# Sixteen gate steps moved beside the first exponentials of an S4 + SwiGLU kernel

## The chip, the cores and the metric

The kernel runs on one core of a Trainium2 chip. It is one launch: forward and backward pass of a block with a state-space layer (S4) and a gated feed-forward layer (SwiGLU). Time is device time in microseconds (us), the median of the runs shown. The engines are TensorE (PE, matrix products, with PEld for loading its weights), VectorE (DVE), ScalarE (ACT, activations from tables), GpSimd (POOL) and SyncE (SP, which issues DMAs). Each engine works through its own instructions in the order in which they stand in the program. Products land in PSUM, everything else lives in SBUF (128 partitions) or in DRAM.

## The reference

Sequence length L = 2048, width D = 576, state N = 128, hidden width F = 4608. Cut to what matters:

```python
xn = layernorm(x)                                   # eps 1e-5
logdA = dt * A;  dB = dt * B                        # D x N, complex
P  = exp(logdA[:, :, None] * l)                     # l = 0 .. L-1
K  = einsum("dn,dnl,dn->dl", C, P, dB).real         # the kernel of the convolution
s  = irfft(rfft(xn, 2L) * rfft(K, 2L))[:L] + xn * Dskip
h  = silu(xn @ w1) * (xn @ w3)                      # gate and up products
out = x + s * silu(h @ w2)
# outputs: out, and the gradients of 12 inputs for a given grad_out
```

## The kernel before

**Stages.** The program has five stretches. (1) Set-up: loads, statistics of the layer norm, selectors and angles. (2) Exponentials: the real part of P is built from powers of a base, so 36 chunks of 16 channels need 54 exponentials of 128x1024 in all; beside them stand the normalisation of x, its transposes, and the spectra of xn. (3) Generation: 36 chunks (`kgen_chunk`, `kgen_sum`) compute sines, multiply them with the exponentials, and sum over N into `KT`. (4) Convolution: two halves (`conv_half`) of four blocks each, products of spectra. (5) The output product (`ffn_output`), the backward pass and the gradients of the inputs.

**The gate steps.** `ffn_hidden` computes gate and up products in 72 steps: 9 blocks of 512 hidden channels (`fb`) times 8 pairs of token tiles. One step has 20 matmuls (L901 for the four full slices of D, L909 for the 64-row tail of both weights), then on ACT silu (`s_t`, L913), a copy of the first tile's gate (`g_t`, L917) and two copies of the up product (`u_t`, L918), on DVE the copy of the second tile's gate (L915) and the product `h_t` (L920). SP stores `h_t`, POOL's queue stores `g_t` and `u_t` for the backward pass. `g_t`, `u_t`, `s_t` and `h_t` have three buffers each, the PSUM tiles `pg` and `pu` two.

**What sets the order.** A scheduler places every instruction by a priority, a time in microseconds written in the source: `pre(us)` in the prologue (us × 600) and `at(us)` after it (100000 + us × 1000). `Chain` makes the instructions of DVE, ACT and POOL in the prologue follow each other in the order written. `ffn_hidden` draws chunks from the generator `ssm_forward` whenever their time is due (`due <= T`), so that a gate step every 6 units of `at` (48 for the 8 of a block) stands against a chunk every 8. The pools of `ffn_hidden` are opened after the prologue has closed its own.

**The prologue.** `ln_load` reads even token tiles straight; odd ones are needed with their rows reversed, so they go through a DRAM copy `odd["A_u"]`, written reversed by one DMA and read back. `ln_stats` takes statistics of all 16 tiles, then one square root on ACT. `ln_normalise` transposes 8 tiles at a time into `ln_pt`; a DMA doubles the last 64 rows. `early_exps` writes e_ps (L514, two PSUM buffers), the exponential (all recorded at the helper's line L72) writes a third of a 128x3072 tile `E_k` (three buffers), and SP stores 18 of these. `early_spectra` computes 128 products of 288 columns (L533, `u_ps`) and DVE copies them (L537). `split3` writes values split into three bfloat16 pieces to `PCS_dram`; those of the base rows come back as `lhs_r`, the operand of the e_ps products. POOL computes the weights Wr and Wi of the sum. `dft_phases` wraps angles on DVE. In generation, L589 and L590 are the products and sines of a chunk (`et_ps` to `cs_k`), L626 its sum (`kps`), L630 the copy to `KT`, one per chunk. In the convolution, ACT copies spectra of KT into `kraw` (L729) and inverse transforms into `ev` (L843), and DVE multiplies.

The core of a gate step (q is the tile of the pair):

```python
nc.scalar.activation(out=s_t[:, :, q, :], in_=pgv, func=ACT.Silu)                      # L913
if q % 2 == 1:
    nc.vector.tensor_copy(out=g_t[:, :, q, :], in_=pgv)                                # L915
else:
    nc.scalar.copy(out=g_t[:, :, q, :], in_=pgv)                                       # L917
nc.scalar.copy(out=u_t[:, :, q, :], in_=pu[:]...)                                      # L918
# after both tiles
nc.vector.tensor_tensor(out=h_t[:]..., in0=s_t[:], in1=u_t[:], op=ALU.mult)            # L920
```

Of the kernel before, what the change touches and what calls it, by code (L numbers as in the profile page):

```python
# [76 lines left out]
class K:  # L77

# [47 lines left out]
    def setup_consts(self):  # L126
# [8 lines left out]
        self.eps_col = const.tile([P, 1], FP32, name="eps_col")  # L135
        nc.vector.memset(self.eps_col[:], 1e-5)
# [8 lines left out]
    def pre(self, us):  # L145
        self.tc.cur_priority = int(us * 600)
# [9 lines left out]
    def ln_load(self, sb):  # L156
        nc, cfg = self.nc, self.cfg
        xf = self.aps["A_u"].flatten_outer_dims()
        self.xs, self.xts = [], []
        for b in range(cfg.LT // 4):  # L160
            xt = sb.tile([P, 4, cfg.D], BF16, name=f"xt{b}")
            rows = xf[4 * b * P:4 * (b + 1) * P, :].rearrange("(i two p) d -> two p i d", two=2, p=P)
            nc.sync.dma_start(out=xt[:, 0:4:2, :], in_=rows[0])
            self.xs += [xt[:, i, :] for i in range(4)]
            self.xts.append(xt)
        for b, xt in enumerate(self.xts):
            nc.sync.dma_start(out=xt[:, 1:4:2, :], in_=self.odd["A_u"][2 * b:2 * b + 2].rearrange("i p d -> p i d"))

    def ln_stats(self, sb, small):
        nc, cfg = self.nc, self.cfg  # L170
        D, LT = cfg.D, cfg.LT
        half = D // 2
        self.mv = sb.tile([P, LT, 2], FP32, name="mv")
        for i in range(LT):
            stats = small.tile([P, 2, 6], FP32, name="stats")
            self.V.bn_stats(stats[:, 0, :], self.xs[i][:, 0:half])
            self.V.bn_stats(stats[:, 1, :], self.xs[i][:, half:D])
            if i > 0:
                self.V.bn_aggr(self.mv[:, i - 1, :], last[:])
            last = stats  # L180
        self.V.bn_aggr(self.mv[:, LT - 1, :], last[:])
        sd = sb.tile([P, LT], FP32, name="sd")
# [3 lines left out]
    def ln_normalise(self, sb, ps):  # L186
        nc, cfg = self.nc, self.cfg
        D, LT, DT = cfg.D, cfg.LT, cfg.DT
        nfull = D // P
        rem = D - nfull * P  # L190
        negmr = sb.tile([P, LT], FP32, name="negmr")
        self.V.scalar_tensor_tensor(out=negmr[:], in0=self.mv[:, :, 0], scalar=-1.0, in1=self.rstd[:], op0=ALU.mult,
                                       op1=ALU.mult)
        TB = 8
        for tb in range(0, LT, TB):
            for i in range(tb, tb + TB):
                self.V.tensor_scalar(out=self.xn_bf[:, i, :], in0=self.xs[i], scalar1=self.rstd[:, i:i + 1],
                                        scalar2=negmr[:, i:i + 1], op0=ALU.mult, op1=ALU.add)
            if tb > 0:
                self.dft_rows()  # L200
            tsl = slice(tb * P, (tb + TB) * P)
            for c, (do, dsz) in enumerate(cfg.dch):
                pt = ps.tile([P, TB * P], BF16, name="ln_pt")
                for j in range(TB):
                    nc.tensor.transpose(pt[:dsz, j * P:(j + 1) * P], self.xn_bf[:, tb + j, do:do + dsz],
                                        self.ident_bf[:])
                self.V.tensor_copy(out=self.xnT[:dsz, c, tsl], in_=pt[:dsz, :])
            nc.sync.dma_start(out=self.xnT[rem:P, nfull, tsl], in_=self.xnT[0:rem, nfull, tsl])
        for b in range(LT // 4):
# [54 lines left out]
    def prologue(self, matp, selp, xp):  # L264
# [6 lines left out]
        self.rstd = self.persist.tile([P, LT], FP32, name="rstd")  # L271
        self.xnT = xp.tile([P, DT, L], BF16, name="xnT")
        self.PCS_dram = self.dram.tile([3, 3, D, N], BF16, name="PCS_dram")
        mul = lambda e, o, a, b: e.tensor_tensor(out=o[:], in0=a[:], in1=b, op=ALU.mult)
        with pool(name="par_tmp", bufs=1) as tmp, pool(name="sel_tmp", bufs=1) as st, pool(name="ln_sb", bufs=1) as lsb, \
                pool(name="ln_small", bufs=4) as small, pool(name="dftgen", bufs=1) as dg, \
                pool(name="ex_l", bufs=1) as lp, pool(name="ex_e", bufs=3) as ep, pool(name="ex_u", bufs=2) as up, \
                pool(name="ex_ps", bufs=2, space=PS) as eps, ExitStack() as early:
            lps = early.enter_context(pool(name="ln_ps", bufs=2, space=PS, side="right"))
            self.V, self.S, self.G = (Chain(self.tc, e) for e in (nc.vector, nc.scalar, nc.gpsimd))  # L280
            self.pre(0)
            irow = st.tile([P, 512], I32, name="irow_i")
            nc.gpsimd.iota(irow[:], pattern=[[1, 512]], base=0, channel_multiplier=0)
            self.dma_engines, self._dma_i = [nc.sync, nc.scalar], 0
            self.odd = {n: self.dram.tile([LT // 2, P, D], BF16, name="odd_" + n) for n in ("A_u", "grad_out", "out_0", "out_1")}
            logdt = self.load_dvec(tmp, aps["A_log_dt"], "logdt", fill=0.0)
            nc.sync.dma_start(out=self.odd["A_u"][:], in_=self.turned(aps["A_u"].flatten_outer_dims()))
            self.pre(0.5)
            self.A_re = self.load_dmat(tmp, aps["A_A_re"], "A_re", fill=-1.0)
            self.ln_load(lsb)  # L290
            self.pre(1)
            SELR = self.selector_values(st)
            LR_ = lp.tile([P, D // 16, N], BF16, name="lhs_r")
# [3 lines left out]
            self.dt_col = self.persist.tile([P, DT], FP32, name="dt_col")  # L297
            self.pre(3)
            self.S.activation(out=self.dt_col[:], in_=logdt_f[:], func=ACT.Exp)
            self.dma_engines = [nc.sync]  # L300
            self.load_rates(tmp)
            self.selector_casts(st)
            dt_b = self.dt_col[:, :, None].to_broadcast([P, DT, N])
# [4 lines left out]
            self.S.copy(out=self.irow[:], in_=irow[:])  # L308
            self.dft_angles()
            for k, eng in enumerate((nc.sync, self.S, nc.sync)):  # L310
                ld = eng.dma_start(out=LR_[k * 16:(k + 1) * 16],
                                   in_=self.PCS_dram[2, k].rearrange("(k p) n -> p k n", p=16))
            self.pre(8)
            self.build_reader(SELR, st)
            self.pre(10)
# [1490 lines left out]
```

## Time and profile before

| what | us |
|---|---|
| median of 3 runs | 1880.09 |
| lowest and highest run | 1870.91 and 1883.1 |
| the profiled execution's own time | 1874.95 |
| its span, first to last instruction | 1873.2 |
| set-up | 0 to 36 |
| exponentials, until the first gate product | 36 to 127.0 |
| until the first sine of generation | 127.0 to 152.3 |
| generation, until the last copy to KT | 152.3 to 433.8 |
| convolution, until the last h_t | 433.8 to 602.3 |
| output product, backward, gradients | 602.3 to 1873.2 |

| engine | busy us | share of the span |
|---|---|---|
| PE | 1689.1 | 90% |
| DVE | 1370.1 | 73% |
| ACT | 910.0 | 49% |
| POOL | 352.1 | 19% |

How to read it: the profile shows one execution. Its span leaves out 1.75 us around the first and last instruction. An instruction is named by engine, line and the tiles that it writes and reads ("PE L901 pg<-wmB_w,xnT"). Groups give count, busy time, mean duration in ns and the idle time of the engine just before them with what ended it. Ends of matmuls are modelled, so that a busy PE need not be a PE at its peak; starts are recorded. Stage borders in the first table are starts and ends of named instructions, so they can be read off the same events in another profile.

### The profile page before, as it was taken

The numbers are of one execution on the slowest core, as the hardware profiler recorded it, in microseconds if no ns is written. First come the engines' busy times: TensorE is split into PE (matmuls) and PEld (weight loads), VectorE is DVE, ScalarE is ACT, GpSimd is POOL, SyncE is SP. The second block draws the span as 40 slices with busy tenths as digits, with TensorE's granted clock in tenths as the row PEclk, the third lists the DMA queues.
The fourth block names the chain that finished last, engine by engine and source line by source line (L and its number), as shares of the span: only waits on it lengthen the run. The fifth ranks groups of instructions, "written<-read, shape, count | busy, mean of one in ns | idle before, by whom it ended". The sixth has DMA issues, their size and how long they took to land. (4 is left out here: it accounts for less than half of the span.)

```text
span 1873.2 us, 38325 instructions
## 1 busy us (share of the span) xinstructions
PE 1689.1 (90%) x15461; PEld 1231.2 (66%) x15516; DVE 1370.1 (73%) x2081; ACT 910.0 (49%) x1632; POOL 352.1 (19%) x567
## 2 busy tenths in 40 slices
PE   2999999999897999799999999999998968979997
PEld 0335555555353777578878887888777756868786
DVE  5538666768988555588694989759998954867675
ACT  3768888887563111465765756565444300001001
POOL 4021222222223111011111111111110242031032
PEclk9999999999998999899999999999999998989999
DMA  6579988887777997658666575579999899988993
GB/s 172 175 242 328 328 304 305 308 291 267 239 242 225 218 205 179 218 157 232 183 198 190 180 211 173 167 210 284 258 233 232 179 221 245 209 195 204 220 210 72
DMA packets 627231, 417.27 MB, mean 223 GB/s; under 512 B 424429, under 2 KB 567853, under 8 KB 622445
## 3 DMA queue, kind: packets, MB, share of 16 engines
q1 hardware_dynamic: 569820, 281.98, 58.3%
q0 software_dynamic: 30672, 106.50, 16.8%
q10 hardware_dynamic: 26560, 26.35, 4.7%
q8 instruction: 121, 1.98, 0.4%
q14 instruction: 58, 0.47, 0.1%
HBM read 135.74 MB, written 190.89 MB: 174 GB/s over the span
## 5 line engine op out<-in xcount | busy, mean ns | idle before, releaser
L1657 PEld LDWEIGHTS <-acts 128*128 128x128 bf16 x2304 | 228.4, 100 | 100.7 <-DMA acts<-GG_dram 19.8
L1610 PEld LDWEIGHTS <-xn_bf 128*128 128x128 bf16 x2304 | 225.6, 98 | 37.0 <-issue 10.1
L1229 DVE TENSOR_TENSOR pr_q<-et_ps,pz 128x1024 f32<-128x1024 f32 x144 | 176.0, 1222 | 48.9 <-PE et_ps L1224 41.8
L1657 PE MATMUL px<-wT,acts 128*128 128x288 bf16 x1408 | 182.5, 289 | 17.3 <-DMA wT<-in_B_w_dram 17.3
L901 PEld LDWEIGHTS <-xnT 128*128 128x128 bf16 x1152 | 107.4, 98 | 115.5 <-issue 25.3
L1232 DVE TENSOR_REDUCE S_all<-pr_q 128x32 f32<-128x1024 f32 x144 | 175.3, 1217 | 3.4
L1552 PE MATMUL ph<-w2T,goT 128*128 128x256 bf16 x1440 | 173.0, 275 | 1.6 <-ACT gh L1555 1.4
L901 PE MATMUL pg<-wmB_w,xnT 128*128 128x512 bf16 x526 | 147.9, 382 | 16.4 <-DVE g_t L915 9.5
L901 PE MATMUL pu<-wmB_w,xnT 128*128 128x512 bf16 x571 | 155.4, 379 | 0.4
L1590 PE MATMUL pgw<-go_o,h_n 128*128 128x288 bf16 x1152 | 150.4, 287 | 4.1 <-DVE h_n L1530 2.8
L1552 PEld LDWEIGHTS <-goT 128*128 128x128 bf16 x1440 | 140.4, 99 | 19.7 <-issue 2.8
L1610 PE MATMUL pgw<-gu_n,xn_bf 128*128 128x256 bf16 x1152 | 135.6, 276 | 7.0 <-ACT gw L1594 6.8
L1657 PE MATMUL px<-wA,acts 128*128 128x288 bf16 x896 | 123.4, 298 | 19.6 <-DMA acts<-GG_dram 19.1
L1590 PEld LDWEIGHTS <-h_n 128*128 128x128 bf16 x1152 | 112.6, 98 | 32.5 <-DVE h_n L1530 3.3
L1610 PE MATMUL pgw<-gg_n,xn_bf 128*128 128x256 bf16 x1152 | 130.2, 273 | 1.6 <-ACT gw L1612 1.6
L913 ACT ACTIVATE s_t<-pg 128x512 bf16<-128x512 f32 x144 | 87.8, 610 | 89.4 <-PE pu L909 44.7
L1685 ACT ACTIVATE go<-gx 128x576 bf16<-128x576 f32 x16 | 10.9, 683 | 220.7 <-DVE gx L1668 220.7
L1555 ACT CAST gh<-ph 128x512 bf16<-128x512 f32 x144 | 82.0, 600 | 71.6 <-PE ph L1552 54.0
L590 ACT ACTIVATE cs_k<-et_ps 128x512 bf16<-128x512 int16 x216 | 112.1, 643 | 1.7 <-PE et_ps L589 1.3
L1612 ACT CAST gw<-pgw 128x256 bf16<-128x256 f32 x144 | 53.9, 375 | 99.3 <-PE pgw L1610 96.7
L924 POOL DMA_DIRECT2D G_dram<-g_t x72 | 52.3, 727 | 232.3 <-DVE g_t L915 223.9
L918 ACT CAST u_t<-pu 128x512 bf16<-128x512 f32 x144 | 86.9, 604 | 12.0 <-PE pu L901 12.0
(302 smaller groups left out, 3232.2 us busy)
## 6 DMA issues: line engine op xcount, KB each, us to landing
U_dram<-u_t POOLq DMA_DIRECT2D x72, 256.0 KB, 4.3
G_dram<-g_t POOLq DMA_DIRECT2D x72, 256.0 KB, 4.0
H_dram<-h_t SPq DMA_DIRECT2D x72, 256.0 KB, 4.7
Q_dram<-q_k SPq DMA_DIRECT2D x36, 512.0 KB, 4.2
h_n<-U_dram POOLq DMA_DIRECT2D x18, 1024.0 KB, 8.7
gg_n<-G_dram POOLq DMA_DIRECT2D x18, 1024.0 KB, 5.9
GU_dram<-gu_n SPq DMA_DIRECT2D x36, 512.0 KB, 3.6
GG_dram<-gg_n SPq DMA_DIRECT2D x36, 512.0 KB, 8.3
```

Of the source, the lines that this page charges most:

```text
L590: nc.scalar.activation(out=CS[:, :, o:o + 256], in_=pt[:].bitcast(I16)[:, :, 0::2], func=ACT.Sin, scale=6.283184 / 2 ** 16)
L901: ins = nc.tensor.matmul(pt[:], lhsT=xnT[:, c, ts], rhs=wm[w][:, c, :], start=(q == 0 and c == 0), stop=(q == 1 and c == nfull - 1))
L913: nc.scalar.activation(out=s_t[:, :, q, :], in_=pgv, func=ACT.Silu)
L918: nc.scalar.copy(out=u_t[:, :, q, :], in_=pu[:].rearrange("p (g f) -> p g f", g=ng))
L1229: nc.vector.tensor_tensor(out=pr[:].rearrange("p r k e -> p r (k e)"), in0=T[h][:].rearrange("p k z d a -> p (k z d a)")[:, None].to_broad ...
L1232: nc.vector.tensor_reduce(out=self.S_all[:, :, d0:d0 + 4], in_=pr[:].rearrange("p r k (d a) -> p (r k) d a", d=4), op=ALU.add, axis=AX.X)
L1552: self.pe_last = nc.tensor.matmul(ph[j][:, k, :].rearrange("p (a f) -> p a f", f=P), lhsT=lw, rhs=rh, start=(n == 0), stop=(n == nfull))
L1555: self.sc(lambda: nc.scalar.copy(out=gh[:, j], in_=ph[j][:]))
L1590: self.pe_last = nc.tensor.matmul(pgw[pi_][:, 0:pw], lhsT=hn[:, tt, fl * P:(fl + 1) * P], rhs=go_o[:, tt, po:po + pw], start=(tt == 0), st ...
L1610: self.pe_last = nc.tensor.matmul(pw_[:, 0:FG], lhsT=self.xn_bf[:, tt, c * P:(c + 1) * P], rhs=nat[:, tt, :], start=(tt == 0), stop=(tt == ...
L1612: self.sc(lambda: nc.scalar.copy(out=gw[:, c], in_=pw_[:, 0:FG]))
L1657: self.pe_last = nc.tensor.matmul(px[pi_][:, 0:pw], lhsT=act[:, ai, fi, :], rhs=w[:, po:po + pw], start=(n == 0), stop=(n == len(steps) - 1))
```

## The change

- **Gate steps among the exponentials.** `EARLY = 16`: the pools of `ffn_hidden` are opened ahead of the prologue, and its first 16 steps are placed among the exponentials; from step 4 on, the first product of step n follows the product of exponential 4n − 13. For block 0 the token tiles are taken in another order (even ones first), weights come over POOL's queue, and the stores of g and u go in one DMA for each of two groups of channels. The later 56 steps are tied to marks: 38 over the 36 chunks (the first ahead of chunk 0), 9 in each half of the convolution.
- **Silu by tanh in these steps.** silu(g)·u = (0.5 + 0.5·tanh(g/2))·g·u: ACT computes tanh into a float32 tile, POOL the product g·u, DVE the rest. All sines, and silus of later steps, are ordered after the last exponential.
- **g copies.** Steps 0 to 3 and those in the convolution have both g copies on ACT; the other early ones have both on DVE; in between, DVE takes q = 1 and a third of q = 0.
- **Layer norm.** Odd tiles are loaded straight and reversed by a product with a flipped identity and copied back by ACT; the DRAM copy of x moves to the start of generation. Statistics, root and normalisation are done for even tiles, then for odd ones; the root is a bit trick with three Newton steps on DVE, so ACT's square root is gone. Tail rows are transposed twice by matmuls instead of doubled by a DMA. Transposes, flips and spectra share a pool of two one-bank PSUM tiles (`t_ps`).
- **Exponentials.** One PSUM buffer instead of two, tiles of 128x1024 with four buffers, 54 stores instead of 18, `E_dram` laid out by pairs of chunks. Spectra are copied in pieces of 288 columns (64 instead of 32 casts).
- **Queues.** The writes of the base rows and their return go over ACT's queue, the other pieces of `split3` over SP's (were POOL's); `dft_phases` moves from DVE to POOL; `load_rates` comes later. Priorities of the prologue (× 1000 instead of × 600), of generation and of the convolution's blocks are new.

The diff, cut to its core:

```diff
-        self.tc.cur_priority = int(us * 600)
+        self.tc.cur_priority = int(us * 1000)
...
+    def ln_flip(self, ps):
+        for t in range(1, self.cfg.LT, 2):
+            for h in range(2):
+                cols = self.xs[t][:, h * H:(h + 1) * H]
+                pt = ps.tile([P, 512], FP32, name="t_ps")
+                nc.tensor.matmul(pt[:, 0:H], lhsT=self.flip_bf[:], rhs=cols, start=True, stop=True)
+                self.S.copy(out=cols, in_=pt[:, 0:H])
...
-        self.S.activation(out=sd[:], in_=self.mv[:, :, 1], func=ACT.Sqrt, bias=self.eps_col[:], scale=1.0)
-        self.V.reciprocal(out=self.rstd[:], in_=sd[:])
+        self.root(small, self.rstd[:, sl], self.mv[:, sl, 1], len(tiles))
...
+    def root(self, small, y, var, n):
...
+        for _ in range(3):
+            V.scalar_tensor_tensor(out=a[:], in0=y, scalar=-0.5, in1=y, op0=ALU.mult, op1=ALU.mult)
+            V.tensor_tensor(out=a[:], in0=a[:], in1=v[:], op=ALU.mult)
+            V.scalar_tensor_tensor(out=y, in0=a[:], scalar=1.5, in1=y, op0=ALU.add, op1=ALU.mult)
...
-                pool(name="ex_l", bufs=1) as lp, pool(name="ex_e", bufs=3) as ep, pool(name="ex_u", bufs=2) as up, \
-                pool(name="ex_ps", bufs=2, space=PS) as eps, ExitStack() as early:
+                pool(name="ex_l", bufs=1) as lp, pool(name="ex_e", bufs=4) as ep, pool(name="ex_u", bufs=2) as up, \
+                pool(name="ex_ps", bufs=1, space=PS) as eps, pool(name="t_ps", bufs=2, space=PS) as tps:
...
-            self.dma_engines, self._dma_i = [nc.sync, self.S], 0
+            self.dma_engines, self._dma_i = [self.S], 0
             self.split3(tmp, rho, 2)
...
+            self.ln_flip(tps)
+            self.dft_sines()
+            even, odd = [*range(0, LT, 2)], [*range(1, LT, 2)]
+            self.pre(12)
+            self.ln_stats(even, small)
+            self.ln_normalise(even, tps)
+            self.early_exps(SELR, LR_, ep, eps, 0, 2)
+            self.pre(24)
+            self.ln_stats(odd, small)
+            self.ln_normalise(odd, tps)
...
-            self.dma_engines = [nc.gpsimd]
+            self.dma_engines = [nc.sync]
             self.split3(tmp, thr, 0)
             self.split3(tmp, th64, 1)
...
+            self.early_spectra(up, tps, 46, 1.1)
+            self.exps_last = self.S.prev
+            for n in range(self.EARLY + 1):
+                next(gate)
...
-            E = ep.tile([P, 2, TW], BF16, name="E_k")
...
+                E = ep.tile([P, 1024], BF16, name="E_k")
                 pe = ps.tile([P, 1024], FP32, name="e_ps")
...
+                self.exps.append(self.e_last)
+                self.S.activation(out=E[:], in_=pe[:], func=ACT.Exp)
+                nc.sync.dma_start(out=self.E_dram[c2 // 2, :, o:o + 1024], in_=E[:])
...
+            with self.tc.issue_after(self.exps_last.ins):
+                nc.scalar.activation(out=CS[:, :, o:o + 256], in_=pt[:].bitcast(I16)[:, :, 0::2], func=ACT.Sin,
+                                     scale=6.283184 / 2 ** 16)
+        self.marks.append(ins)
...
+    def gate_mark(self, n):
+        i = n - self.EARLY
+        if i < 38:
+            return 36 * i // 38 - 1
+        h, k = divmod(i - 38, 9)
+        return 36 + 8 * h + (-1 if k == 0 else (1, 3, 4, 4, 5, 5, 6, 6)[k - 1])
...
+            ld = nc.sync if fb else nc.gpsimd
...
+                pair = [4 * (n % 4) + n // 4 + 2 * q for q in range(NT)] if fb == 0 else [NT * n, NT * n + 1]
+                early = step < self.EARLY
...
+                                        if early:
+                                            lead = self.exps[4 * step - 13] if step >= 4 else None
+                                        else:
+                                            lead = self.marks[mark] if mark >= 0 else None
...
-                    nc.scalar.activation(out=s_t[:, :, q, :], in_=pgv, func=ACT.Silu)
-                    if q % 2 == 1:
+                    if early:
+                        nc.scalar.activation(out=th[:, :, q, :], in_=pgv, func=ACT.Tanh, scale=0.5)
+                    else:
+                        with self.tc.issue_after(self.exps_last.ins):
+                            nc.scalar.activation(out=s_t[:, :, q, :], in_=pgv, func=ACT.Silu)
+                    if step < 4 or step >= self.EARLY + 38 or (not early and q == 0 and step % 3):
+                        nc.scalar.copy(out=g_t[:, :, q, :], in_=pgv)
+                    else:
                         nc.vector.tensor_copy(out=g_t[:, :, q, :], in_=pgv)
...
+                if early:
+                    nc.gpsimd.tensor_tensor(out=s_t[:], in0=g_t[:], in1=u_t[:], op=ALU.mult)
+                    nc.vector.tensor_scalar(out=hv, in0=th[:], scalar1=0.5, scalar2=0.5, op0=ALU.mult, op1=ALU.add)
+                    nc.vector.tensor_tensor(out=hv, in0=hv, in1=s_t[:], op=ALU.mult)
+                else:
+                    nc.vector.tensor_tensor(out=hv, in0=s_t[:], in1=u_t[:], op=ALU.mult)
...
-            k.prologue(matp, selp, xp)
+            gate = k.ffn_hidden(wp, gup, fps)
+            k.prologue(matp, selp, xp, gate)
...
-                k.ffn_hidden(wp, gup, fps, 0, 12, k.ssm_forward(0, 8, 8))
+            k.ssm = k.ssm_forward(21, 7.3, 1)
+            for _ in gate:
+                pass
```

More of the change, by code (lines that the diff above doesn't have):

```diff
@@ L169, in ln_stats @@
[L169 to L174, printed above, removed]
+        self.xts = [sb.tile([P, 4, cfg.D], BF16, name=f"xt{b}") for b in range(cfg.LT // 4)]
+        for k in range(2):
+            for b, xt in enumerate(self.xts):
+                rows = xf[4 * b * P:4 * (b + 1) * P, :].rearrange("(i two p) d -> two p i d", two=2, p=P)
+                nc.sync.dma_start(out=xt[:, k:4:2, :], in_=rows[k])
@@ new lines, in ln_load, with ln_stats @@
+        self.xs = [xt[:, i, :] for xt in self.xts for i in range(4)]
+    def ln_flip(self, ps):
+        nc, H = self.nc, self.cfg.D // 2
+        for t in range(1, self.cfg.LT, 2):
[4 more added lines that the diff above has]
+                self.S.copy(out=cols, in_=pt[:, 0:H])
+    def ln_stats(self, tiles, small):
+        half = self.cfg.D // 2
+        last = None
+        for i in tiles:
@@ L210, in ln_normalise, with ln_fold @@
+    def ln_fold(self):
+        for b in range(self.cfg.LT // 4):
             lo, hi = self.xn_bf[:, 4 * b:4 * b + 2, :], self.xn_bf[:, 4 * b + 3:4 * b + 1:-1, :]
```

315 lines of the change are left out of this document (166 added, 149 removed).

## The prediction

> **What bounds the kernel now.** I first read the page's busy digits in 40 slices of 46.8 us, then busy time in windows cut at events of the trace, then the timelines and groups inside them.
>
> ```profile
> PE   2999999999897999799999999999998968979997
> DVE  5538666768988555588694989759998954867675
> ACT  3768888887563111465765756565444300001001
> ```
>
> TensorE (PE) is at 9 nearly throughout, but that is one reading over stages with different limits. The windows (us, busy time and instruction count per engine, granted clock, DMA share, GB/s) are: exponentials, generation of the kernel, convolution, and everything after.
>
> ```profile
> 36.00:127.00 91.00, 85.17 (x271) 26.42 (x270) 39.33 (x73) 65.45 (x69) 12.83 (x17) 1.00 0.58 197
> 152.30:433.80 281.50, 272.10 (x3599) 153.09 (x3635) 199.82 (x276) 244.21 (x485) 68.25 (x94) 1.00 0.89 310
> 433.80:602.30 168.50, 148.72 (x836) 76.70 (x849) 157.66 (x216) 94.04 (x197) 39.67 (x54) 0.96 0.73 237
> 602.30:1873.00 1270.70, 1157.80 (x10625) 962.28 (x10622) 931.67 (x1401) 486.55 (x853) 210.00 (x371) 0.97 0.81 204
> ```
>
> Between the first and second lie 25.3 us, up to the first sine. PE bounds generation (272 of 281.5), VectorE (DVE) the convolution (157.7 of 168.5). The exponentials also look PE-bound, but that PE is slow. In PE's timeline (start, duration, count):
>
> ```profile
> 126.05 1.14 PE L533 MATMUL u_ps<-xt,cCS 128*128 128x288 bf16 x4
> 126.98 0.63 PE L901 MATMUL pg<-wmB_w,xnT 128*128 128x512 bf16 x1
> ...
> 130.01 1.04 PE L901 MATMUL pg<-wmB_w,xnT 128*128 128x512 bf16 x4
> ...
> 134.11 1.04 PE L901 MATMUL pg<-wmB_w,xnT 128*128 128x512 bf16 x4
> ...
> 136.06 0.65 PE L533 MATMUL u_ps<-xt,cCS 128*128 128x288 bf16 x4
> ```
>
> The same four 288-column products take 1.14 us before the first gate product at 126.98 and 0.65 after it; single starts lie 240 ns apart before 127. The window prints clock 1.00, yet these spacings are half speed: the printed clock can't be used there. So 85 us of PE work is about 43 at full rate, and ACT waits for it:
>
> ```profile
> ACT E_k L72 <- PE e_ps L514: 40.5, 37, 17.2
> ```
>
> **Part 1: generation loses gate steps.** A gate step (two token tiles, 20 products) is 130.01 to 134.11, 4.10 us of PE. Of 72, three finish before 152.3, 45 in generation, 24 after (counted by h_t). Copies of KT mark chunks:
>
> ```profile
> L630 ACT CAST KT<-kps x3: 402/403/403, 250.2 to 267.7; 128x256 bf16<-128x256 f32 x3
> ```
>
> They start at 250.20, 256.96 and 267.72: a chunk with one gate is 6.76 us, with two 10.76, so a further gate is 3.95 to 4.1. Check: 36 × 6.8 + 9 × 3.95 = 280.4, measured 281.5. The changed order holds 17 gates ahead of the first sine, 37 among the 36 chunks and 18 in the convolution. Hence 36 × 6.8 + 3.95 = 248.8, **−32**. The bound below: DMA moves 281.5 us × 310 GB/s = 87 MB here; 8 steps fewer take off 8 × 0.77 MB, and 81 MB at those 310 GB/s would need 262 us, −20. Two slices of the page reach 328, which gives 247, so I keep −32. The bound above is chunks at 2.7 + 4.0 throughout, −34. Late next is ACT: 244.2 less 8 gates × 3.0 (two each of 0.61, 0.60 and one of 0.58) = 220 of 249, and DVE, which takes over every third first g copy, 199.8 + 12 × 0.68 − 8 × 1.35 = 197; PE stays last.
>
> **Part 2: the convolution loses gate steps and copies.** DVE pays for every gate:
>
> ```profile
> L915 DVE CAST g_t<-pg 128x512 bf16<-128x512 f32 x24 | 16.2, 677 | 1.2 <-ACT s_t L913 1.2
> L920 DVE TENSOR_TENSOR h_t<-s_t,u_t 128x1024 bf16<-128x1024 bf16 x24 | 16.1, 671 | 0.3 <-ACT u_t L918 0.3
> ```
>
> Six gates fewer save 6 × 1.35 = 8.1 us, the g copies moved to ACT 18 × 0.68 = 12.2: 20.3. DVE then holds 137 us, plus its 11 of waits, so 148 to 150: I take **−18**. ACT gains 18 × 0.58 and loses 6 × 3.0, 94 to 86; PE falls to 149 − 24 = 125; neither binds. The bounds are −25 (the new places also fill DVE's waits of 5.1 and 3.5 us for kraw and KT) and −10 (ACT copies delay kraw and ev, for which DVE waits already).
>
> **Part 3: the prologue gains gate steps.** Its end, the first sine, is now at 152.3.
> - PE at full rate: 17 × 4.1 = 70; 54 pairs of exponents × 0.45 = 24; 128 spectra products × 0.12 = 15.6; transposes and flips 7; W 1.4: 118 us. Products could begin when the even half is normalised: its statistics are half of 15.2 us, root 13 × 0.16 = 2.1 (by DVE's smallest rows, 0.15 to 0.19), eight at 0.42; with the loads about 40. So 158 if PE never waits.
> - ACT: 54 × 1.025 = 55.4; 16 × 2 tanh at silu's 0.61 and 2 u copies at 0.60 = 38.8; g copies of four steps 4.7; W 4.5; one table load 1.3: 105 from about 46, so 151. The two engines are close; neither fully hides the other.
> - DVE: before's 39 + later g copies 12 × 2 × 0.68 = 16, plus h work 16 × (0.68 + 0.68) = 22, plus smaller casts and early statistics: about 96, covered by 125.
> - Two exponent buffers become one: a pair then waits for the exponential before it. Such a turn-round has no row; lower bound 0 (ACT does a tanh or a copy meanwhile), upper 0.8 × 54 = 43 (pair 0.45 plus hand-over). Most exponentials alternate with gate work; 5.
> - POOL gets a product 128x1024, estimated 1.39 × 1024/640 = 2.2 us from its W products, plus 2 to 4 DMA issues of 0.73: at most 5.1 of each step's about 7, covered. W's eight products (11 us) and the selectors stand in its order between two gates' stores: with three g_t buffers a stall of 0 to 10; 4.
> - SP carries 54 stores of 256 KB instead of 18 of 768, the H stores, spectra, and split pieces moved from POOL. An H store waits for DVE, which waits for POOL; exponential stores stand behind it, four buffers deep, then the exponential itself. 0 if on time, 48 if each of 16 costs 3 us; 3.
> - Gone: the square root (1.28 + 0.31), a DRAM turn of x ahead of statistics, and a tail DMA. All inside the 40 above; the turn itself (8 × 128 × 576 elements of 2 bytes = 1.2 MB, against 87 MB there) moves to generation's start, where nothing waits for it before the output product. Exponent rows and their DMAs go to ACT's queue; behind them stand only exponentials that need them anyway: 0. Sine and silu wait for the last exponential; behind them on ACT stand generation's copies, which need that sine anyway.
>
> 158 + 5 + 4 + 3 ≈ 170, less 2 because generation's first loads are issued earlier: first sine at 168, **+16**. Bounds: 148 (−4, ACT's sum with starts at 43) and 195 (+43, turn-round in full).
>
> **A rule against it.** Row: POOL's gxs products, 128x576, take 1.27 to 1.28 us with no two-input DVE operation beside them; no row has such an overlap. The Trainium skill, "SBUF — State Buffer", section "Who interferes with whom", says that a DVE instruction with two SBUF inputs and a GpSimd one that reads SBUF exclude each other for the whole instruction. By it 16 × 2.2 = 35 us of DVE's prologue could be closed to such operations; with 29 us slack my estimate is up to 6 us later, 1847.
>
> **Sum.** −32 − 18 + 16 = −34. Everything after 602.3 keeps 1270.7 us. Against the profiled execution's 1874.95 that is **1841**; the median of the runs, 1880.09, is 5 above that execution, which I leave to the range.
>
> **Rivals.**
> *Slower: PE stays at half speed in the prologue.* For: 70 us of almost unbroken work left it at 240 ns spacing, and in the change each gate is again surrounded by that work. Against: the first gate products turned the clock 1.3 us after 126.98, and four spectra products between later gates ran in 0.65. Price: 118 × 2 from 40, so first sine 276, +124 − 50 = **1949**. It decides against the gain from a first sine at 202, when 37% of the work runs slow. Chance 0.11. The Trainium skill, "TensorE: Matmul & The Clock Gate", section "What's actually happening", has some 3.4 us of sustained activity warm it, whatever the product; the trace disagrees for exponents and spectra, so I don't lean on it.
>
> *Same: in-order queues hold the prologue* (SP or POOL stall of 3 us per gate, as above): first sine 152.3 + 48 = 200, **1873**. For: POOL's PCS_dram issue already waits 62.7 us for DVE in before. Against: four store buffers. Chance 0.14.
>
> *The convolution keeps its length*, since the late wait is kraw or ev behind ACT copies: **1859**. Chance 0.12.
>
> *The gates don't move:* the built order has 16 complete ones among the exponentials, and table loads only at sine, exponential and silu, none around tanh. Excluded.
>
> **Numbers.** Forecast 0.63, its own range 1812 (−4 − 34 − 25) to 1868. Its upper corner is 1888 (+43 − 20 − 10), which needs three upper bounds at once. The range 1812 to 1880 takes in the third rival and most of the second; outside lie the first and the tails, 0.2. One per cent of 1880 is 19 us, about what measurement can tell from no change: faster is below 1861. Faster: forecast 0.60, third rival 0.08, second 0.02 = 0.70. Same: 0.03 + 0.04 + 0.09 = 0.16. Slower: 0.11 + 0.03 = 0.14.
>
> **What would show it.** Spacing of 288-column products near 120 ns from the first gate on; first sine near 168; about 250 us from there to the last KT copy; about 150 to the last h_t, with DVE still busiest; 1270 behind. It is wrong if the spacings stay 240, if ACT waits before exponentials for their store buffers, or if DVE waits for kraw grow by what its copies gave.

## The result and the profile after

The changed kernel takes 1951.84 us (median of four runs, 1942.72 to 1956.64) against 1880.72 before: 1.038 times, 95% interval 1.033 to 1.044. The profiled execution took 1956.64, 81.7 more than that of before. Cut at the same events as before (first exponent product, first sine, last copy to KT, first output product), with columns as before (us, busy time and count per engine, granted clock, DMA share, GB/s), the windows of the changed kernel are:

```profile
35.00:226.40 191.40, 151.85 (x693) 56.87 (x706) 118.05 (x227) 109.48 (x156) 89.83 (x78) 0.86 0.58 195
226.40:481.30 254.90, 243.72 (x3472) 143.41 (x3508) 198.32 (x284) 223.65 (x446) 58.16 (x80) 1.00 0.88 309
481.30:648.00 166.70, 123.85 (x689) 64.91 (x700) 138.92 (x183) 82.18 (x179) 36.71 (x50) 0.87 0.73 210
648.00:1954.90 1306.90, 1166.14 (x10630) 966.92 (x10630) 931.43 (x1400) 486.03 (x853) 203.28 (x363) 0.96 0.82 198
```

| stretch | before | after | forecast | measured |
|---|---|---|---|---|
| until the first sine | 152.3 | 226.4 | +16 | +74.1 |
| generation | 281.1 | 254.9 | −32 | −26.2 |
| convolution, until the first output product | 168.1 | 166.7 | −18 | −1.4 |
| everything after | 1271.7 | 1306.9 | 0 | +35.2 |
| sum | | | −34 | +81.7 |

Most of the loss is in the prologue; 35.2 us more lie behind the output product's start, which was forecast to keep its length, and the two stretches that were to pay for it gave back less or nothing. The forecast ended the convolution with the last h_t. In before that stands within 1 us of the first output product; in the changed kernel it starts at 636.0, 12 us ahead of it. By the forecast's own border the convolution is 14 us shorter and everything after 48 longer. In the 40 slices (now of 48.9 us) the clock's row dips in the prologue, and PE's row has holes there and in the convolution:

```profile
PE   3678999999976699979999999999769985979897
DVE  5965587777986355678696798849779973777575
ACT  3536898888654011166665756655335410100101
PEclk9869999999988799989999999999889997989999
```

Of the changed prologue's 191 us, 54.6 stand at half speed in the profile's records of the granted clock. And in its waits no engine stands out: PE, ACT, DVE and POOL wait for each other.

```profile
POOL G_dram L1011 <- ACT g_t L991: 39.0, 2, 31.2
...
ACT E_k L72 <- PE e_ps L541: 31.8, 23, 6.2
DVE g_t L993 <- ACT th L986: 31.2, 17, 6.5
...
PE t_ps L561 <- DVE u_e L565: 17.9, 14, 5.0
DVE h_t L1000 <- POOL s_t L998: 15.7, 10, 2.3
```

The median of before lies 5.8 us above its profiled execution, that of the changed kernel 4.8 below, so 81.7 in the profiles stands for 71 in the medians. The profiled executions of a_epsx2 and a_w_d below are more than 1.5% longer than the fastest of these kernels, so only their prologues are read.

### The profile page after: what moved, and what is told of

It reads as the page before. It is cut to its first block, busy times and chain, and to the rows that moved or that the text cites. A ratio compares the mean times of both kernels' runs of the same rounds, so it can differ in the third digit from the quotient of the medians.

```text
span 1954.9 us, 38582 instructions
## 1 busy us (share of the span) xinstructions
PE 1687.7 (86%) x15487; PEld 1232.9 (63%) x15548; DVE 1406.8 (72%) x2161; ACT 909.5 (47%) x1644; POOL 405.8 (21%) x596
## 5 line engine op out<-in xcount | busy, mean ns | idle before, releaser
L1696 PEld LDWEIGHTS <-xn_bf 128*128 128x128 bf16 x2304 | 226.7, 99 | 44.6 <-issue 16.6
L1315 DVE TENSOR_TENSOR pr_q<-et_ps,pz 128x1024 f32<-128x1024 f32 x144 | 176.1, 1223 | 53.9 <-PE et_ps L1310 44.9
L973 PE MATMUL pg<-wmB_w,xnT 128*128 128x512 bf16 x523 | 153.8, 400 | 8.5 <-issue 6.6
L1696 PE MATMUL pgw<-gu_n,xn_bf 128*128 128x256 bf16 x1152 | 137.9, 278 | 13.9 <-ACT gw L1680 13.7
L1743 PE MATMUL px<-wA,acts 128*128 128x288 bf16 x896 | 117.5, 289 | 17.8 <-DMA acts<-GG_dram 13.9
L1007 POOL DMA_DIRECT2D G_dram<-g_t x64 | 46.4, 726 | 327.8 <-DVE g_t L993 185.1
L1698 ACT CAST gw<-pgw 128x256 bf16<-128x256 f32 x144 | 53.9, 375 | 100.9 <-PE pgw L1696 94.8
L1681 POOL DMA_DIRECT2D out_dram<-gw x36 | 20.0, 555 | 386.9 <-ACT gw L1680 325.3
L989 ACT ACTIVATE s_t<-pg 128x512 bf16<-128x512 f32 x112 | 69.3, 618 | 59.3 <-PE pu L981 20.2
```

The costliest lines, as they stand in the source:

```text
L973: ins = nc.tensor.matmul(pt[:], lhsT=xnT[:, c, ts], rhs=wm[w][:, c, :], start=(q == 0 and c == 0), stop=(q == 1 and c == nfull - 1))
L1007: nc.gpsimd.dma_start(out=dst[fb * ng:(fb + 1) * ng, :, tsl, :].rearrange("g p t f -> p g (t f)"), in_=src[:].rearrange("p g t f -> p g (t ...
L1315: nc.vector.tensor_tensor(out=pr[:].rearrange("p r k e -> p r (k e)"), in0=T[h][:].rearrange("p k z d a -> p (k z d a)")[:, None].to_broad ...
L1696: self.pe_last = nc.tensor.matmul(pw_[:, 0:FG], lhsT=self.xn_bf[:, tt, c * P:(c + 1) * P], rhs=nat[:, tt, :], start=(tt == 0), stop=(tt == ...
L1698: self.sc(lambda: nc.scalar.copy(out=gw[:, c], in_=pw_[:, 0:FG]))
L1743: self.pe_last = nc.tensor.matmul(px[pi_][:, 0:pw], lhsT=act[:, ai, fi, :], rhs=w[:, po:po + pw], start=(n == 0), stop=(n == len(steps) - 1))
```

## The experiments

First theory: the gates fill the prologue, held up by the single exponent buffer. Rivals: POOL's work shuts out DVE; PE runs at half clock. "First sine" is read from each kernel's trace, the time from its runs against before on the same chip.

| kernel | first sine | recorded half clock before it | median | ratio to before, interval |
|---|---|---|---|---|
| before | 152.3 | no record before 128.3 | | |
| changed | 226.4 | 54.6 | 1951.84 | 1.038 (1.033 to 1.044) |
| a_early3 | 223.4 | 149.0 | 1962.55 | 1.042 (1.031 to 1.052) |
| a_epsx2 | 221.4 | 47.8 | 1938.42 | 1.029 (1.019 to 1.039) |
| a_wearly | 212.8 | 37.5 | 1936.22 | 1.030 (1.022 to 1.038) |
| a_dvemul | 207.4 | 30.7 | 1927.18 | 1.025 (1.015 to 1.035) |
| b_eps1 | 175.1 | 53.9 | 1927.56 | 1.026 (1.018 to 1.033) |
| a_e512 | 223.8 | 47.8 | 1939.99 | 1.033 (1.025 to 1.040) |
| a_w_d | 198.3 | 20.5 | 1923.82 | 1.021 (1.012 to 1.030) |
| a_e512_w_d | 191.8 | 13.7 | 1918.39 | 1.020 (1.013 to 1.027) |
| b_rows128 | 133.4 | 17.0 | 1872.56 | 0.996 (0.993 to 0.999) |
| b_gact | 150.8 | 61.4 | 1873.22 | 0.997 (0.993 to 1.001) |
| a_w2late | 228.5 | 54.6 | 1947.00 | 1.036 (1.030 to 1.042) |
| a_all | 191.2 | 13.7 | 1907.89 | 1.016 (1.011 to 1.020) |
| e3_rows128 | 209.5 | 105.4 | 1941.41 | 1.034 (1.029 to 1.039) |
| a_rows128 | 224.6 | 44.4 | 1934.62 | 1.032 (1.028 to 1.036) |
| b_rows_gact | 134.9 | 20.5 | 1853.35 | 0.988 (0.985 to 0.992) |

**a_early3.** Three early gate steps, 45 among the chunks, 24 in the convolution.

```diff
-    EARLY = 16
+    EARLY = 3
...
-        if i < 38:
-            return 36 * i // 38 - 1
+        if i < 45:
+            return 36 * i // 45 - 1
```

> Only three gate steps stand in the prologue again (before has three), 45 among the chunks and 24 in the convolution; everything else of the change stays, so its prologue with tanh, single exponent buffer and even tiles first is seen almost without gates. Theory 'gates' (the 13 further steps fill the prologue's engines): first sine back to about 155 (226 in the changed kernel, 152 in before), generation about 281, total within 15 us of before. Theory 'one exponent buffer' (each exponential and the pair before it in series, about 0.74 us of ACT idle between two exponentials): most of it is paid without gates too, 54 x 1.77 = 96 us from 46, and with eight WT copies and a table load the first sine comes at about 150 to 165. Theory 'POOL and tile reuse': no gate stores and products in POOL's order, so its part, about 20 us, is gone.

Without 13 of the gates the first sine comes only 3 us earlier, at 223.4: what stands there without them is as long. That does not make the gates' work free. PE now spends 146 us of its 174 us of exponentials at half clock, and 149 of the whole prologue against 54.6 with sixteen gates, so this run changed two things at once: the gates and the clock. The convolution, with 24 gates as before, took 156.3.

**b_eps1.** The opposite side: before, with one part of the change.

```diff
-                pool(name="ex_ps", bufs=2, space=PS) as eps, ExitStack() as early:
+                pool(name="ex_ps", bufs=1, space=PS) as eps, ExitStack() as early:
```

> The kernel before with one exponent buffer in place of two, nothing else. Theory 'one exponent buffer': pair and exponential in series at half clock take 2.16 us (seen at 128 to 131 in the changed kernel) and spectra products of 0.24 us stand between them in PE's order, 54 x 2.16 + 128 x 0.24 = 148 from 36.6, so the last exponential near 185 instead of 126, first sine near 205, total 1875 + 50 to 60 = about 1930. Theory 'the rest of the new prologue' (even and odd halves, POOL, flips): last exponential within 10 us of 126.

The last exponential came at 161.4 (126.2 in before), the first sine at 175.1: +23 where +53 was expected. The buffer costs, but it is not the +74 alone. The median, 1927.56, came out as expected (about 1930) all the same, by luck: in the profile 34.6 us of its loss lie behind the output product's start, as in the changed kernel, and 6.7 in generation.

**a_epsx2 and a_e512.** Two buffers back in the changed kernel, paid for with PSUM of the gates, or by halving them.

```diff
-                pool(name="ex_ps", bufs=1, space=PS) as eps, pool(name="t_ps", bufs=2, space=PS) as tps:
+                pool(name="ex_ps", bufs=2, space=PS) as eps, pool(name="t_ps", bufs=2, space=PS) as tps, \
+                pool(name="f_ps_e", bufs=1, space=PS) as self.fps:
```

> Two exponent buffers of two PSUM banks as in before; paid for by one buffer each of pg and pu in the prologue (two afterwards, as now). Theory 'one exponent buffer': ACT's idle 0.74 us between two exponentials goes, up to 54 x 0.74 = 40 us, first sine at 226 - 30 to 40 = 186 to 196, total about 1915. Theory 'POOL and tile reuse': the stalls from 95 to 133 stay, first sine 220 or later. If the gates' own PSUM were the limit, it gets later than 226.

```diff
-                pool(name="ex_ps", bufs=1, space=PS) as eps, ...
+                pool(name="ex_ps", bufs=2, space=PS) as eps, ...
...
-                pe = ps.tile([P, 1024], FP32, name="e_ps")
                 for k in range(2):
...
+                    pe = ps.tile([P, 512], FP32, name="e_ps")
...
+                    self.S.activation(out=E[:, 512 * k:512 * k + 512], in_=pe[:], func=ACT.Exp)
-                self.S.activation(out=E[:], in_=pe[:], func=ACT.Exp)
```

> The changed kernel with the exponent's two banks used as two buffers of 512 columns, each with an exponential of its own (108 of 128x512 instead of 54 of 128x1024); PSUM, gates and stores as in the changed kernel. Theory 'one exponent buffer': ACT's idle of 0.74 between exponentials goes, first sine 226 - 20 to 35 = about 191 to 206. Theory 'POOL and in-order spectra': the stalls before 135 stay and eat most, first sine 215 or later. If 512-column exponentials cost 0.2 us more per 1024, 10 us of the gain are lost.

First sines 221.4 and 223.8: 5.0 and 2.6 us. The theory of the buffer as the main term falls; in a_epsx2 ACT instead waited 36.1 us for the gates' products, whose buffers had been given up.

**a_wearly and a_dvemul.** POOL's part. In the first, the calls that build the selectors and W move ahead of `ln_flip`; in the second:

```diff
-                    nc.gpsimd.tensor_tensor(out=s_t[:], in0=g_t[:], in1=u_t[:], op=ALU.mult)
+                    nc.vector.tensor_tensor(out=s_t[:], in0=g_t[:], in1=u_t[:], op=ALU.mult)
```

> POOL's selector and W products are moved in front of the first gate, where POOL idles from 22 to 53 in the changed kernel. Theory 'POOL and tile reuse' (DVE operations of 0.5 to 1.9 us last 1 to 3.7 us while POOL computes, DVE waits 5.1 us for a tile that W still uses, and PE's spectra products, ahead of exponents in PE's order, wait for DVE): the stall of ACT between 95 and 108 goes, first sine 12 to 25 us earlier, 201 to 214. Theory 'one exponent buffer': no more than 5 us.

> The product of gate and up of the 16 early steps is made by DVE (0.68 us each) instead of POOL (2.13 each). Theory 'POOL and tile reuse' in the form that POOL's product shuts DVE out: the stretched DVE operations from 57 to 66 shorten by about 5 us, and DVE's wait for POOL's product (15.7 us in ten places) goes; first sine 5 to 15 us earlier. Theory 'one exponent buffer': first sine within 4 us of 226, because ACT and not DVE sets the pace from 141 on.

They gave 13.6 and 19.0 us, the largest single edits. One way in which POOL does it is seen in the timelines of POOL, DVE and PE of the changed kernel (start, duration, operation; in brackets idle time before it):

```profile
58.94 2.13 POOL L998 TENSOR_TENSOR s_t<-g_t,u_t 128x1024 bf16<-128x1024 bf16 x1
...
64.02 2.13 POOL L998 TENSOR_TENSOR s_t<-g_t,u_t 128x1024 bf16<-128x1024 bf16 x1
```

```profile
57.45 3.66 DVE L72 TENSOR_SCALAR rt_v<-mv 128x8 f32<-128x8 f32 x1
61.14 2.12 DVE L72 TENSOR_SCALAR rt_a<-rt_v 128x8 int32<-128x8 int32 x1
...
64.20 1.97 DVE L72 TENSOR_TENSOR rt_a<-rt_a,rt_v 128x8 f32<-128x8 f32 x1
66.21 0.17 DVE L72 SCALAR_TENSOR_TENSOR rstd<-rt_a,rstd 128x8 f32<-128x8 f32 x1
```

```profile
68.80 0.73 PE L217 MATMUL t_ps<-ident_bf,xn_bf 128*128 128x128 bf16 x4 [8.78 <-DVE xn_bf L72]
```

An operation on 8 columns, 0.17 us in the last line, takes 3.66 and ends at 61.11, 0.04 after POOL's product (58.94 + 2.13 = 61.07); the one at 64.20 ends at 66.17, POOL's second product at 66.15. PE's transposes wait 8.8 us for the normalisation behind them. Counted against the shortest of its kind in the traces, 15 DVE operations of the changed prologue are stretched by about 21 us in all, none in before. In a_w_d 13 are still stretched, by 12 us in all, but eleven of them lie between 23 and 38 us, ahead of the first gate. The rule of the Trainium skill ("SBUF — State Buffer", "Who interferes with whom") agrees with the two-input operation at 64.20; the section also lets operations with one input, `tensor_scalar` among them, shut GpSimd out or be shut out in some modes, and the forecast had left these aside, though the two longest here are of that kind. The forecast's estimate of at most 6 us was too small, because stretched operations lay on the path. How much of the two edits' gain is this stretching, how much DVE's waits for POOL's product (15.7 us in ten places) and how much W's place in POOL's order, the runs do not separate.

**a_w_d and a_e512_w_d.** Both, and both with the half-size buffers.

> Both POOL edits together: selectors and W ahead of the gates, and the product of gate and up on DVE. Alone they gave first sines of 212.8 and 207.4 (226.4 without). If they remove different stalls: about 194. If it is the same stall: about 207.

> All three: two half-size exponent buffers, early selectors and W, product on DVE. If buffer and POOL stalls are separate terms, first sine near 226 - 32 - 25 = 169, which is the 168 of the prediction, and total about 1895; if one hides behind the other, 185 to 195 and about 1915.

First sines 198.3 (28.1 us earlier: mostly different stalls) and 191.8. With POOL out of the way the buffers are worth 6.5. What is left is PE itself, in the window of a_e512_w_d from its first exponential to its first sine:

```profile
46.20:191.80 145.60, 137.41 (x650) 48.39 (x648) 104.78 (x229) 105.93 (x196) 36.52 (x50) 0.95 0.76 252
```

PE is busy 137 of 146 us. From 41.7 the distances between the starts of its products add up to 82 us for 17 gates and the beginning of one more (4.7 each), 37.8 for 118 products into e_ps (0.62 a pair of exponents among other products, 0.68 with PE's waits) and 29.6 for spectra and transposes. A gate step costs PE no less here than among the chunks, where it is 3.95 to 4.1; there was little idle PE to use.

**b_rows128.** The exponent products contract over 48 rows. Here they contract over all 128, the other 80 filled with zeros; the columns are the same.

```diff
+            nc.gpsimd.memset(LR_[:], 0.0)
...
-                    self.e_last = nc.tensor.matmul(..., lhsT=LR_[0:48, c2 + ch, :], rhs=SELR[0:48, o1:o1 + 512],
+                    self.e_last = nc.tensor.matmul(..., lhsT=LR_[:, c2 + ch, :], rhs=SELR[:, o1:o1 + 512],
```

> The kernel before with the exponent products over all 128 rows: the 80 rows that were left out hold zeros in lhs_r, so the result is the same and the columns streamed are the same 512. Theory 'clock by filled rows' (the clock stays at half through 70 us of unbroken work because two thirds of that work are 48-row products): 288-column products are 120 ns apart soon after 40 us, exponentials take 0.62 + spectra instead of 1.03, last exponential near 100 to 110 instead of 126, total 1878 - 15 to 25. Theory 'clock by the kind of stage' (waits on ACT, whatever the rows): spacing stays 240, total unchanged within 5.

PE's timeline in it:

```profile
86.19 0.59 PE L515 MATMUL e_ps<-SELR,lhs_r 128*128 128x512 bf16 x2
86.62 0.41 PE L534 MATMUL u_ps<-xt,cCS 128*128 128x288 bf16 x2
87.11 0.59 PE L515 MATMUL e_ps<-SELR,lhs_r 128*128 128x512 bf16 x2
87.53 0.65 PE L534 MATMUL u_ps<-xt,cCS 128*128 128x288 bf16 x4
```

Four 288-column products now take 0.65 us, 19 us before the first gate product, where before needed 1.14; a pair of exponents takes 0.43 instead of 0.96. The last exponential comes at 103.5 instead of 126.2. So in before it was the products over 48 rows, more than half of PE's busy time between 57 and 127 (38 of 68 us), that kept the clock at half, through 70 us almost without a gap. b_gact, whose prologue is that of before and whose records begin at 61.8, has half clock from 65.2 to 126.7, until 1 us behind its first gate product. Whether the few rows do it by themselves or the alternation of 48-row with 128-row products, which the edit takes away too, is not shown. The Trainium skill ("TensorE: Matmul & The Clock Gate", "What's actually happening") counts only sustained activity; the trace of before disagrees. In the medians the gain is 0.4%: the stretch behind the output product's start is 25 us longer in this profile than in before's.

**e3_rows128 and a_rows128.** The same edit in the changed kernel, with three and sixteen gates.

> The changed kernel with three early gate steps, and the exponent products over 128 rows (80 of them zeros). That kernel without the 128 rows spent 134 us of its prologue at half clock and reached the first sine at 223. If the clock makes that time: half clock below 40 us and first sine near 46 + 54 x 1.77 + 15 = 155 to 170. If the single buffer makes it at any clock: first sine above 195.

> The changed kernel with the exponent products over 128 rows, nothing else. In it 54.6 us of the prologue ran at half clock, worth at most 27 us. If half clock comes from the 48-row products: first sine 200 to 208, half clock below 20 us. If it comes from PE's own waits (for DVE's spectra copies and for the exponential before): half clock stays above 40 us and first sine above 218.

First sines 209.5 (from 223.4) and 224.6 (from 226.4); half clock still 105 and 44 us (from 149, not the 134 of the expectation, and 54.6). ACT's timeline of e3_rows128 shows why the rows don't settle it here:

```profile
154.35 1.02 ACT L72 ACTIVATE E_k<-e_ps 128x1024 bf16<-128x1024 f32 x1 [0.73 <-PE e_ps L542]
156.12 1.02 ACT L72 ACTIVATE E_k<-e_ps 128x1024 bf16<-128x1024 f32 x1 [0.74 <-PE t_ps L562]
...
185.72 1.02 ACT L72 ACTIVATE E_k<-e_ps 128x1024 bf16<-128x1024 f32 x1 [1.15 <-PE e_ps L542]
187.89 1.02 ACT L72 ACTIVATE E_k<-e_ps 128x1024 bf16<-128x1024 f32 x1 [1.15 <-PE e_ps L542]
```

With one buffer an exponential comes every 1.76 us at full clock and every 2.17 at half, and at half clock PE is busy less than half of the time. So there seem to be two ways to half clock: few filled rows (before), and PE's own waits (one buffer, the changed prologue). In the changed kernel the second fits: the 128 rows took only 10 of its 54.6 us, the two POOL edits of a_w_d 34. That PE's waits are the cause is argued from this; no run changes them alone.

**b_gact and a_w2late.** The convolution.

```diff
-                    if q % 2 == 1:
+                    if q % 2 == 1 and fb * LT + i0 < 96:
```

> The kernel before with one part of the change alone: in the 24 convolution steps both g copies are made by ACT. Theory of the prediction (DVE sets the pace of the convolution, a copy costs it 0.68): 24 x 0.68 = 16 us less DVE, convolution 156 instead of 168 as in the kernel with three early steps, total 1878 - 12. Rival: ACT's copies delay kraw and ev, convolution within 4 us of 168.

From the last KT copy to the first output product b_gact took 159.0 us instead of 168.0: the copies on ACT are worth 9.0 here, so DVE does set that pace; in the medians the gain is not clear of no change (0.993 to 1.001). Why the changed kernel kept 166.7 shows in DVE's timeline and in SP's:

```profile
605.04 0.45 DVE L883 TENSOR_TENSOR s_t<-ev,et_ps 128x288 bf16<-128x288 f32 x1 [15.40 <-DMA S_dram<-s_t]
```

```profile
559.53 5.11 SPq L1489 DMA_TRANSPOSE hcA<-H_dram  x1
...
579.76 19.88 SPq L1575 DMA_TRANSPOSE hcA<-H_dram  x1
```

```profile
580.09 2.26 POOL L1040 DMA_DIRECT2D w2a<-in_B_w_dram  x3 [4.20 <-PE et_ps L763]
```

The transposing load of H for the output product (into one of three buffers, hcA, hcB and hcC; first line: before, where four loads of w2 were issued 12 to 18 us ahead of it; second line: changed) now begins with the loads of w2; it takes 19.9, the stores of S behind it land after 18.5, and DVE, out of S buffers, waits 15.4. In a_w2late the loads of w2 follow the last store of u:

```diff
-                ld = nc.gpsimd.dma_start(out=w2g, in_=aps["B_w2"]...)
+                with self.tc.issue_after(self.last_store.ins):
+                    ld = nc.gpsimd.dma_start(out=w2g, in_=aps["B_w2"]...)
```

> The changed kernel with the loads of w2 put behind the last store of u in POOL's order (they are at 580 in it, the moment hcA's transposing load of H begins). Theory 'collision': the store of S lands in 5 instead of 18 us, DVE's wait of 15.4 and PE's of 15.3 us go, convolution about 152 instead of 167, and hcA takes 5 instead of 20. Rival: hcA's load is slow by itself (it reads rows that were just written), convolution stays at 165 or more, and the late w2 delays the output product.

hcA took 5.39 us and the convolution 151.5, 15.2 less. The profiled time fell by 12.7 us, the median by only 5, which the intervals don't tell from nothing. The collision has moved: w2 now meets the third such load, and the stretch behind, 1307.2 us, is as long as in the changed kernel:

```profile
581.86 5.39 SPq L1576 DMA_TRANSPOSE hcA<-H_dram  x1
624.44 22.10 SPq L1576 DMA_TRANSPOSE hcC<-H_dram  x1
```

**a_all.** The four helpful edits in the changed kernel.

> Two half-size exponent buffers, early selectors and W, product of gate and up on DVE, and late w2 together. If the terms add up: first sine 192 (as with the first three), generation 255, convolution 152, total 1918 - 15 = about 1903, still slower than before, because PE has no idle time left in the prologue and a gate step costs it as much there as among the chunks.

1907.89, with first sine 191.2, generation 255.0 and convolution 152.8 as expected, and slower than before.

**b_rows_gact.** The version that the experiments point to: before, with b_rows128's and b_gact's edits and without any gate moved.

> The kernel before with the two edits that helped it alone: exponent products over 128 rows (first sine 19 us earlier) and both g copies of the convolution on ACT (convolution 9 us shorter). If they add: first sine 133, convolution 159, 28 us less up to the output product, total about 1850 to 1860, faster than both kernels. If the convolution's gain only lets a transposing load of H collide later, 1862 to 1870.

```profile
36.10:134.90 98.80, 78.09 (x401) 37.61 (x407) 55.69 (x104) 75.89 (x93) 17.30 (x22) 0.90 0.72 248
134.90:416.00 281.10, 271.72 (x3597) 152.90 (x3633) 199.83 (x276) 243.82 (x484) 68.07 (x94) 1.00 0.88 308
416.00:575.10 159.10, 145.17 (x829) 74.87 (x843) 143.80 (x192) 103.07 (x222) 41.56 (x57) 0.98 0.77 256
```

The gains add up to the output product, which begins at 575.1 instead of 601.5, and the time is 1853.35 against 1874.86, 0.988 (0.985 to 0.992): 1.2% faster than before and faster than the changed kernel. Its third load of H takes 19.6 us (6.8 in before), so a slow transposing load is there too.

## Why the prediction was wrong

**First sine, +16 forecast, +74 measured: the failed step.** The prediction gave the prologue 158 us of PE from 40, plus 12 for three kinds of stalls, less 2. What the runs put in its place:
- *PE's sum.* With the stalls taken away the first sine still comes at 191.8. Of the prices, a pair of exponents was 0.45 by halving the cold row and measured 0.62 (0.43 with 128 rows), 0.68 with PE's waits, 12 us too little; a gate was 4.1 by its row in one piece and measured 4.7 where it is cut into by other products (13.7 us of the prologue still at half clock included), 12 us too little; transposes and spectra 7; the remainder is the start at 41.7, 4 us from the last exponential to the sine, and rounding.
- *POOL.* Taken at 4 us, with an estimate of up to 6 from two-input operations alone; the two edits gave 28.1. The part on W was named (its products between the gates' stores), but not that DVE's chain and, in PE's order, the spectra and the exponents behind them hang on it.
- *The exponent buffer.* Taken at 5; 6.5 by the last step of a_e512_w_d. About right here, though worth 22.8 by itself in before (b_eps1): beside gates PE uses the turn-round.

The sum of these, 191.8 + 6.5 + 28.1, is the measured 226.4, by the edits' order; other orders would share it differently.

**Generation, −32 forecast, −26 measured.** The pace was right: most KT copies are 6.8 us apart. The price of a moved gate stands. Missed were 8.3 us from the first sine to the first copy, five of the first intervals at 7.0 to 7.8, and 9.1 for the last. The check that the prediction made on before came out by luck: its 10.3 us to the first copy were made up by two short intervals behind it, 4.6 and 2.6.

**Convolution, −18 forecast, −1.4 measured (−14 to the last h_t).** The mechanism was right: 151.5 without the collision is −16.6, and DVE is busy 138.9 us where 137 was forecast. The step that failed is the silent assumption that the transposing load and w2 would stay apart as in before. The rival "keeps its length" named ACT's copies; it was a DMA.

**After the output product, 0 forecast, +35.2 measured.** The silent assumption was that unchanged instructions keep their times. PE's stand in the same order, but SP now loads hcC ahead of hcB, which PE needs first; hcB's load takes 16.3 us, beside loads of w2, and PE waits 6.8 us for it. This is part of 12.5 us lost up to the backward pass's first product. The other 22.6 come behind it; near 1390 and 1440 pairs of transposing loads of the weights take 24.8 and 18.2 us (8 each in before):

```profile
1313.16 8.06 SPq L1489 DMA_TRANSPOSE wA<-in_B_w_dram  x2
...
1378.34 24.81 SPq L1575 DMA_TRANSPOSE wA<-in_B_w_dram  x2
...
1304.39 21.70 SPq L1490 DMA_TRANSPOSE wA<-in_B_w_dram  x2
```

The lines are from before, the changed kernel and b_rows128. Such pairs are not the change's alone: b_rows128, which alters nothing there, had 22 and 18 in its profile, b_gact 6 to 9 in each of five, and b_eps1, whose stretch is 34.6 us longer than in before, 17 in one. What makes them slow in one execution and not in another stays open; it may also be why b_rows128's 19 us shrank to 5 in the medians.

**The slower rival, 1949.** Its number lies next to the measured 1951.84, but its mechanism was too strong: the prologue was at half clock for 54.6 us, at most 27 of the 74, not throughout. And the gates it took for the warming agent did warm PE; where there were only three, half clock held 149 us. That fits that moving them cost so little there (226.4 against 223.4) while the rest of the new prologue cost so much. The rival of in-order queues was to show by ACT's wait for the exponentials' store buffers: that came to 0.8 us, once.

## What to carry to other kernels

Before filling "idle" time beside a slow stage, find out why the stage is slow: here it was half clock from 48-row products, and filling their rows with zeros (no further columns) brought the first sine 19 us forward, where filling the time with other work put it back by 74. Price moved work with its row in the mixed order and through every engine that it hands over to, and give an engine that shares a lock (POOL with DVE) or a PSUM buffer a term that can stand on the path. And where a stage ends sooner, list the DMAs which then start together.

## What the runs showed of the hardware

- In before the granted clock went with the rows that the products fill: 70 us of nearly unbroken products, more than half of the busy time over 48 rows, stayed at 240 ns per 288 columns; with 128 rows, 80 of them zero, they ran at 122 ns (b_rows128, half clock 17.1 us in all).
- At full clock a 512-column product over 48 rows took about 0.31 us from start to start when a 128-row product followed (a_e512_w_d) and 0.226 when another of 48 rows did; over 128 rows 0.216 (b_rows128).
- Exponentials of 512 columns followed each other 0.49 us apart, those of 1024 0.92: halving them cost ACT some 0.06 us per 1024 columns (a_e512 and before).
- A DVE operation of 0.17 us lasted 3.66 while POOL issued stores and multiplied, and ended within 0.04 us of POOL's product (changed kernel).
- A transposing DMA load of H took 5.4 us, and 19.9 beside four loads of w2 (2.4 MB): a_w2late and the changed kernel. Others beside loads of w2 took 16.3 and 22.1.
